# Block-sparse attention with a gated convolution: one tile for keys and queries, more buffers, and two segments' output turned on TensorE

## The chip, the cores and the metric

The kernel runs on one core of a Trainium2 chip. Time is device microseconds of that core for one launch, inputs in device memory at the start and the output there at the end. The time before is the median of three runs, 211.81 us (210.3 to 212.96).

The core has five engines that work side by side, each through its own queue in order, and meet at semaphores: TensorE (PE; the loading of its stationary operand is listed as PEld), VectorE (DVE), ScalarE (ACT), GpSimd (POOL) and SyncE (SP). SP and POOL here mainly issue DMAs.

## The reference

Attention of 4 batches x 8 heads, 768 positions, 64 elements a head, with a mask by blocks of 32; its output, heads side by side, goes through a feed-forward layer whose hidden values are gated by a short convolution over positions.

```python
scores = scale * np.matmul(q, k.transpose(0, 1, 3, 2))
mask = np.abs(blk_i - blk_j) <= window                  # neighbours, first and last block,
mask = mask | (blk_i == 0) | (blk_j == 0) | (blk_i == n_blocks - 1) | (blk_j == n_blocks - 1)
# ... and three sampled key blocks for each query block
attn = softmax(np.where(mask, scores, -1e9))
x = np.matmul(attn, v)            # -> (4, 768, 512), heads side by side
h = np.maximum(x @ w_in, 0.0)     # 512 -> 1024
conv_out = sum(conv_w[k] * shift(h, k - 1) for k in range(3))
out = (h * sigmoid(conv_out)) @ w_out
```

## The kernel before, in words

All 768 x 768 scores of a head are computed; the mask is added inside the same matmul, by 24 more rows of the contracted dimension (rows 64 to 87 of the key and query tiles, one row a block).

**Segments and units.** Heads are taken in pairs (16 pairs, named P). A batch has two query segments of 384 positions; the very last is cut in 256 and 128, so there are nine segments (`SEGS`). A segment's attention is cut in units: a unit is eight blocks of 128 keys x 128 queries, 144 units in all. For each unit TensorE computes scores into one of two `st` tiles (L744, two halves of four blocks), ScalarE takes the exponential into a `pt` tile (L755), and TensorE multiplies with the values into `av` (L777), where a column of ones gives the sum. When a pair of heads is done with a segment, VectorE takes the reciprocal of the sums (L694) and normalises into `xtok` (L696, both in `norm_ops`). `xtok` has positions on partitions; the next matmul needs features there, so it is transposed into `xT`: by a DMA through the crossbar, issued from SP (L705), or, for the (segment, pair) listed in `X_PE` (L217), by TensorE (L715) with a copy out of the `mix` tile.

**Feed-forward.** For each segment, 32 matmuls "f1" (L893) into `mix`, a rectifier on ScalarE or VectorE (L913, L915) into `hE`, the convolution as multiplications and additions on VectorE (L947, L957), tanh on ScalarE (L996), the gate on VectorE (L999, L1004) and the matmuls "f2" (L823), whose result goes through `o2s` to the output.

**Keys and queries.** For each pair, the key and query tiles stand as two: `E_t` and `O_t` (L156, L157), each with three blocks of 128 for keys and queries and two heads. A row of the loaded tile `nat` holds neighbouring positions, so the even and the odd of them come out of a transpose on partitions 0 to 63 and 64 to 127, and go to `E_t` and `O_t`. Pairs 0 to 4 are transposed on TensorE (L468, L506) and copied out of PSUM (`cp` in `kq_transposes`, through `dcopy`, L326 and L328); the others through the crossbar into `stg` (L583) and from there with two copies, "stg_cp". A score matmul takes the keys of one block and one or two neighbouring query blocks of the same tile. Slots 1 to 4 get their mask rows from slot 0 by copies on VectorE or DMAs on SP (L359); the last batch's second segment gets its own query rows by DMAs ("m_last", L595).

**Order.** Nothing is scheduled at run time. `put_down` walks the string `ORDER` (L20), which names each operation, the engine it goes to where there is a choice (ScalarE or VectorE for copies and rectifiers), and the buffer it takes; each engine's queue holds its operations in that order. GpSimd issues the loads (L238) with tiny copies "pace" between them (L415, L658) that wait for an exponential or an earlier load, so that loads do not run ahead.

Of the kernel before, what the change touches and what calls it, by code (L numbers as in the profile page):

```python
# [20 lines left out]
040708090506000b1e00a0A0102030e0c0z0d0gV1f1c01q11s11t0WV20f0hA0oA0UAr21r3r4r5r6r7r8r9rarbrcrdrerfrgrhrirjrkrl  # L21
rmrnrorprqrrrsrtru0Y0rv1210ZA00XA0VA0+ArwrxryrzrArBrCrDrErFrGrH0/015110A16A0i0x13V14V0lV0jVrI4o017A0y0mV11V0B
0nA4prJrK4t14q04u1g11hV11j01lV1kV0q0p1dV01E21G31H1801m11S00O1U2461V0t0u0w0v4v11iV4y04z4D14E4A24I04J4F34K44r14s
4w4Q14R4S54x4B4C0s0r1rV14V04W4G1u01vV24+14/4X05011x11zV4H4L1yV4N0530544M05b15c4T0E15525d31wV0C0F1FV25g05h1I04U
5l14Y5i45m1JV34Z1L11KV5n51MV1NV4O5q05r19051525v15w565s05x1571TV30G5810J0N591bV1aV5e15D05E5f5j5k5o5I15J5F25p5t
1n15N05u5y5O5z05G0P470Q48241490R4a1A04b0S4c2604d274e0T4f2c24g1O14h2e14i2f4j2k04k2m34P05a4l2n4m5K35S15H5L5T5P4
5A25B5C1oV5U55/05M605Q6105R6415V5W656906a5X05Y25V41pV5Z05+V6616e16216fhr1ho06b26g36j0hp636khs0k0DhqV0htVhM06l4
6r1676s6t5hx0hyhzA6w06xhu1hv1B06y0hOhNhPhwVhQhU1hVhWhX6B16C686c6d6hhD16G0hE6H1CA1DA6D1hFAhA06i6m6n06O1hB1W16u
6P6v6z6I2hCAhRhY1XV46o1i021YV6pi16Q36T0hG06A6U6E6V4hH6F6Y16ZhJ16J6+56KhK710726R16S6WhZhLAhIA730i3hSi26L0i4hT0
i57611P1im06X6/1RV1QV777e01Z1707f747817j17k756M2806q1296Ni831+V1/Viah+2dV0h/i9ig17g27l37o07p797a07h7i7t17u7q4  # L30
i6ibi77b2ic7v5ih7B07C7D0id7m7n7r7s7G17w7x7Hin2lV12aV0io7L07M2g12h7I17N2ii7c7d7y12bV7z7E17Q17R7F7J7K7V07Wieifip
7O7S37A7X42s12u2v24n0IiqV0811827P7T7U860878358807Y7Z0ij8b18civ0iw8g08h7+02iV12jV2tV2ixV7/ikA1is1itiuViQ08d12o0
# [80 lines left out]
def kernel(  # L113
# [90 lines left out]
    def t_d4(n):  # L204
        return 0.129 + n / 3840.0
# [855 lines left out]
```

## Time and profile before

| | |
|---|---|
| median of three runs | 211.81 us (210.3, 211.81, 212.96) |
| profiled execution: span from first to last instruction | 207.2 us |
| profiled execution: its own time beside the span | not listed apart; the median stands 4.6 us above the span |
| PE / PEld busy | 196.7 / 153.7 us |
| DVE / ACT / POOL busy | 181.5 / 189.4 / 60.7 us |
| exponentials on ScalarE (L755) | 144 of 1036 ns, 140.2 us busy |
| score matmuls (L744) | 900 |
| crossbar transposes of the attention output (SP) | 32 |
| read and written | 23.08 and 6.29 MB |

How to read it: PE's busy time counts matmuls that overlap in its pipeline, so their mean durations hold latency, and distances between starts say more about its rate. PEld runs beside PE. An idle time is put down to what ended last before it. A line can be that of a helper: all plain copies on VectorE are L328, all on ScalarE L326, all loads L238.

### The profile page before, as it was taken

How to read it: one execution, taken by the hardware profiler on the slowest of the kernel's cores; microseconds unless marked ns; L12 is line 12 of the kernel's file. 1: busy time of each engine (PE TensorE's matmuls, PEld its weight loads, DVE VectorE, ACT ScalarE, POOL GpSimd, SP SyncE). 2: the span in 40 equal slices, each digit the busy share in tenths (PEclk: the TensorE clock that was granted, in tenths of full speed). 3: DMA queues.
4: the chain of work that ended last, by engine and by line, in shares of the span. 5: the costliest groups of instructions: out<-in, count | busy, mean ns of one | idle time of the engine just before them, and what ended most of it. 6: DMA issues, size and time to landing. Idle time of an engine off the chain costs nothing.

```text
span 207.2 us, 6783 instructions
## 1 busy us (share of the span) xinstructions
PE 196.7 (95%) x2667; PEld 153.7 (74%) x2687; DVE 181.5 (88%) x571; ACT 189.4 (91%) x248; POOL 60.7 (29%) x113
## 2 busy tenths in 40 slices
PE   7799979989999999999999999999999999999993
PEld 7689858867878877777688767777688877795752
DVE  6877759999699998999999998999799959999950
ACT  6899969999999999999999998999899999998841
POOL 8844355446326124500605292700000000000000
PEclk9999999999999999999999999999999999999999
DMA  6999999999998699993597689992511032100415
GB/s 149 170 207 200 173 169 126 141 135 157 158 151 134 98 138 194 181 190 58 77 167 133 88 103 218 170 213 73 175 43 22 19 121 66 29 11 6 156 50 202
DMA packets 54903, 26.26 MB, mean 127 GB/s; under 512 B 40864, under 2 KB 51832, under 8 KB 54872
## 3 DMA queue, kind: packets, MB, share of 16 engines
q0 software_dynamic: 19984, 11.24, 43.5%
q1 hardware_dynamic: 34312, 13.90, 33.8%
q10 hardware_dynamic: 576, 0.69, 1.0%
q8 instruction: 21, 0.34, 0.7%
q14 instruction: 10, 0.08, 0.2%
HBM read 23.08 MB, written 6.29 MB: 142 GB/s over the span
## 4 chain that ended last, share of the span: by engine, by line
PE 56%; ACT 16%; DVE 16%; DMA 5%; issue 4%; SPq 0%; ACTq 0%
PE st L744 16%; PE mix L893 14%; PE mix L823 14%; ACT pt L755 12%; PE av L777 9%; DVE m L947 5%; DMA xT<-xtok 3%; DVE m L957 3%; DMA o2s<-in_q_dram 2%; DVE hE L915 2%; DVE xtok L696 2%; DVE gT L1004 1%; ACT hE L913 1%; DVE m L999 1%; DVE e L328 1%
## 5 line engine op out<-in xcount | busy, mean ns | idle before, releaser
L755 ACT ACTIVATE pt<-st 128x1024 bf16<-128x1024 f32 x144 | 140.2, 1036 | 5.4 <-PE st L744 5.0
L777 PEld LDWEIGHTS <-pt 128*128 128x128 bf16 x1152 | 53.1, 97 | 11.6 <-issue 0.2
L777 PE MATMUL av<-vt,pt 128*128 128x65 bf16 x1152 | 60.6, 193 | 0.3
L893 PE MATMUL mix<-xT,winb 128*128 128x384 bf16 (+2 forms) x288 | 53.8, 308 | 1.1 <-DMA xT<-xtok 0.9
L947 DVE TENSOR_SCALAR m<-hE,cw 128x382 bf16<-128x382 bf16 (+2 forms) x192 | 49.6, 317 | 0.2
L744 PE MATMUL st<-o 88*128 88x128 bf16 (+1 forms) x240 | 44.3, 229 | 1.1 <-ACT pt L755 0.8
L744 PE MATMUL st<-o,e 88*128 88x128 bf16 (+1 forms) x228 | 43.8, 233 | 0.5 <-ACT pt L755 0.4
L744 PE MATMUL st<-e,o 88*128 88x128 bf16 (+1 forms) x224 | 43.0, 234 | 1.2 <-ACT pt L755 1.2
L823 PE MATMUL mix<-woutb,gT 128*128 128x512 bf16 x156 | 43.1, 379 | 0.8
L744 PE MATMUL st<-e 88*128 88x128 bf16 (+1 forms) x208 | 41.5, 239 | 0.6 <-ACT pt L755 0.5
L744 PEld LDWEIGHTS <-o 88*128 88x128 bf16 x464 | 34.4, 97 | 9.4 <-issue 3.0
L744 PEld LDWEIGHTS <-e 88*128 88x128 bf16 x436 | 33.0, 97 | 7.5 <-issue 1.4
L957 DVE TENSOR_TENSOR m<-m 128x764 bf16<-128x764 bf16 (+2 forms) x64 | 33.8, 532 | 0.4
L893 PEld LDWEIGHTS <-winb 128*128 128x128 bf16 x288 | 23.9, 97 | 8.2 <-issue 1.6
L996 ACT ACTIVATE m<-m 128x764 bf16<-128x764 bf16 (+2 forms) x32 | 26.3, 826 | 0.5 <-DVE m L957 0.4
L415 POOL COPY pace<-pt 1x1 bf16<-1x1 bf16 x24 | 8.3, 347 | 47.3 <-ACT pt L755 47.0
L823 PEld LDWEIGHTS <-gT 128*128 128x128 bf16 x184 | 15.4, 97 | 9.0 <-DVE gT L1004 0.5
L915 DVE TENSOR_SCALAR hE<-mix 128x384 bf16<-128x384 f32 x29 | 15.9, 554 | 4.3 <-PE mix L893 4.1
L696 DVE TENSOR_TENSOR xtok<-av,rcp 128x384 bf16<-128x384 f32 (+2 forms) x36 | 18.2, 506 | 0.3
L1004 DVE TENSOR_TENSOR gT<-m,hE 128x764 bf16<-128x764 bf16 (+3 forms) x36 | 18.1, 508 | 0.3
L913 ACT ACTIVATE hE<-mix 128x384 bf16<-128x384 f32 (+2 forms) x35 | 16.9, 503 | 1.6 <-PE mix L893 1.2
L238 POOL DMA_DIRECT2D nat<-in_q_dram x23 | 16.9, 736 | 3.0 <-issue 2.8
(80 smaller groups left out, 156.4 us busy)
## 6 DMA issues: line engine op xcount, KB each, us to landing
out_dram<-o2s SPq DMA_DIRECT2D x22, 256.0 KB
vn<-in_v_dram POOLq DMA_DIRECT2D x16, 192.0 KB, 5.3
nat<-in_k_dram POOLq DMA_DIRECT2D x15, 192.0 KB, 5.1
nat<-in_q_dram POOLq DMA_DIRECT2D x7, 192.0 KB, 4.8
winb<-in_moe_w_in_dram POOLq DMA_DIRECT2D x2, 512.0 KB, 8.1
woutb<-in_moe_w_out_dram POOLq DMA_DIRECT2D x4, 256.0 KB, 5.8
nat<-in_q_dram POOLq DMA_DIRECT2D x8, 96.0 KB, 5.3
xT<-xtok SPq DMA_TRANSPOSE x32
```

The lines of the kernel that those rows point to most:

```text
L696: nm = op("norm", {"DVE": t_dps(128 * C)}, lambda e: nc.vector.tensor_tensor(out=xtok_t[xk.index][:, 0:C].rearrange("p c h d -> p h c d"), ...
L744: nc.tensor.matmul(out=st[:, 128 * x:128 * (x + n_)], lhsT=QK[kc % 2][s][0:88, 1, hh, kc // 2, :], rhs=QK[par][s][0:88, 0, hh, idx:idx + n ...
L755: nc.scalar.activation(out=pt_t[ptb.index], in_=st_t[stb.index], func=AF.Exp, bias=0.0, scale=0.125)
L777: nc.tensor.matmul(out=o[:, off:off + 65], lhsT=pt_t[ptb.index][:, 128 * x:128 * x + 128], rhs=V_t[vslot_b[P].index][:, hh, kc, 0:65], sta ...
L823: nc.tensor.matmul(out=acc(), lhsT=gT_t[gb.index][:, ffc, 128 * t:128 * t + 128], rhs=woutb[:, ffc, :], start=(ffc == 0), stop=(ffc == NFF ...
L893: nc.tensor.matmul(out=mix_t[hb.index][:, w1 * y:w1 * y + w1], lhsT=winb[:, fc, 128 * ffc:128 * ffc + 128], rhs=xT_t[xt_buf[n].index][:, f ...
L913: i = nc.scalar.activation(out=dst, in_=src, func=AF.Relu, bias=0.0, scale=0.5)
L915: i = nc.vector.tensor_scalar(out=dst, in0=src, scalar1=0.5, scalar2=0.0, op0=ALU.mult, op1=ALU.max)
L947: i = nc.vector.tensor_scalar(out=m_t[cb.index][:, x, y, 0:w], in0=hE_t[heb.index][:, f0 + y, t0 + x:t0 + x + w], scalar1=cw[:, x, f0 + y: ...
L957: nc.vector.tensor_tensor(out=m[:, a_, :, 0:w], in0=m[:, a_, :, 0:w], in1=m[:, b_, :, 0:w], op=ALU.add)
L996: th = [op("tanh", {"ACT": t_act(2 * w) + 0.04}, lambda e, cb=cb, w=w: nc.scalar.activation(out=m_t[cb.index][:, 0, :, 0:w], in_=m_t[cb.in ...
L1004: i = nc.vector.tensor_tensor(out=gT_t[gtb.index][:, f0:f0 + 2, t0:t1], in0=m_t[cb.index][:, 0, :, 0:w], in1=hE_t[heb.index][:, f0:f0 + 2, ...
```

## The change

- Keys and queries of a pair stand in one tile `QK_t` with six blocks; `E_t` and `O_t` become views of every second block. The blocks of a query segment are thereby neighbours (0, 1, 2 and 3, 4, 5), and a score matmul takes up to three of them. Mask rows are copied in fewer, larger pieces; `mlast`'s three parts change places to fit.
- More buffers: `stg` 2 to 3, `nat` 4 to 6, `vn` 3 to 4, `pt` 6 to 8, `xtok` and its sums 3 to 4, `xT` 3 to 4, `o2s` 4 to 5.
- `X_PE` also names all four pairs of segments 0 and 1.
- `ORDER` is another string: other places in the queues, other engines for some copies, other buffers.

```diff
@@ -151,10 +152,10 @@
     av_t = [ps.tile([128, 512], FP32, tag=f"av{x}", name=f"av{x}") for x in range(NAV)]
     mix_t = [ps.tile([128, 512], FP32, tag=f"mix{x}", name=f"mix{x}") for x in range(NMIX)]
 
-    NSLOT, NSTG, NNAT, NVN, NPT, NXK, NXT, NHE, NCV, NGT, NOS = 5, 2, 4, 3, 6, 3, 3, 2, 4, 2, 4
-
-    E_t = many(NSLOT, [88, 2, 2, 3, 128], BF16, "e")
-    O_t = many(NSLOT, [88, 2, 2, 3, 128], BF16, "o")
+    NSLOT, NSTG, NNAT, NVN, NPT, NXK, NXT, NHE, NCV, NGT, NOS = 5, 3, 6, 4, 8, 4, 4, 2, 4, 2, 5
+
+    QK_t = many(NSLOT, [88, 2, 2, 6, 128], BF16, "qk")
+    E_t, O_t = [[t[:, :, :, x:6:2] for t in QK_t] for x in range(2)]
     V_t = many(NSLOT, [128, 2, 6, 66], BF16, "vt")
     stg_t = many(NSTG, [128, 2, 2, 3, 128], BF16, "stg")
     nat_t = many(NNAT, [128, 2, 768], BF16, "nat")
@@ -214,7 +215,7 @@
 
     SW = 0.715
     NWARM = 45
-    X_PE = ((0, 3), (7, 3), (8, 2), (8, 3))
+    X_PE = ((0, 0), (0, 1), (0, 2), (0, 3), (1, 0), (1, 1), (1, 2), (1, 3), (7, 3), (8, 2), (8, 3))
     WOUT_U = (15, 19, 23, 27)
 
 
@@ -316,7 +317,7 @@
         put(to[:, 1:2, :, 5:11], 1)
         mid = to[:, 0:1, :, 6:11]
         a_ = [list(x) for x in mid.ap]
-        put(bass.AP(tensor=mid.tensor, offset=mid.offset, ap=[a_[0], [255, 2], [16, NB // 3], [1, 5]]), 1)
+        put(bass.AP(tensor=mid.tensor, offset=mid.offset, ap=[a_[0], [511, 2], [16, NB // 3], [1, 5]]), 1)
 
     def k_copy(t, h):
         return lambda e: dcopy(e, t[0][64:88, 1, h], E_t[0][64:88, 1, 0])
@@ -334,7 +335,7 @@
     mlast = sb.tile([88, 3, 128], BF16, tag="mlast", name="mlast")
 
     def last_rows(e):
-        for y, (t0, c, n_) in enumerate(((384, 0, 2), (640, 0, 1), (384, 1, 2))):
+        for y, (t0, c, n_) in enumerate(((384, 0, 2), (384, 1, 2), (640, 0, 1))):
             src = nblk[:, t0:t0 + 128 * n_].rearrange("j (p c) -> j c p", c=n_)[:, c]
             if e == "ACT":
                 nc.scalar.activation(out=mlast[64:88, y], in_=src, func=AF.Copy, bias=0.0, scale=-8000.0)
@@ -351,13 +352,12 @@
     mask_ready[(0, 1)] = m_h1 + m_kh
     for s in range(1, NSLOT):
         mr = []
-        for x, t in enumerate((E_t, O_t)):
-            if s < SLOT_DMA:
-                mr.append(op("m_slot", {"DVE": t_d4(1536) + 0.05}, lambda e, t=t, s=s: dcopy(e, t[s][64:88], t[0][64:88]),
-                             T(4.5 * s - 2.5) + 0.1 * x, [m_h1[x], m_kh[x]], earliest=7.0 + 2 * s))
-            else:
-                mr.append(op("m_dma", {"SP": 0.75}, lambda e, t=t, s=s: nc.sync.dma_start(out=t[s][64:88], in_=t[0][64:88]),
-                             T(4.5 * s - 2.5) + 0.1 * x, [m_h1[x], m_kh[x]], dma=("hw", 0.6)))
+        for x, t in enumerate((E_t, O_t) if s < SLOT_DMA else ()):
+            mr.append(op("m_slot", {"DVE": t_d4(1536) + 0.05}, lambda e, t=t, s=s: dcopy(e, t[s][64:88], t[0][64:88]),
+                         T(4.5 * s - 2.5) + 0.1 * x, [m_h1[x], m_kh[x], m_k[x]], earliest=7.0 + 2 * s))
+        if s >= SLOT_DMA:
+            mr = 2 * [op("m_dma", {"SP": 0.75}, lambda e, s=s: nc.sync.dma_start(out=QK_t[s][64:88], in_=QK_t[0][64:88]),
+                         T(4.5 * s - 2.5), m_h1 + m_kh + m_k, dma=("hw", 0.6))]
         mask_ready[(s, 0)] = mask_ready[(s, 1)] = mr
 
     def mask_in(slot, h, kp, par):
@@ -482,7 +482,7 @@
             for x, t in enumerate((E_t, O_t)):
                 def cp(e, t=t, x=x, hs=hs, mb=mb, n=n, bt=bt):
                     src = bt[mb.index].bitcast(BF16)[64 * x:64 * x + 64, 384 * hs[0]:384 * hs[0] + n]
-                    dcopy(e, t[slot.index][0:64, 1, hs[0]:hs[-1] + 1].rearrange("p h c s -> p (h c s)"), src)
+                    dcopy(e, t[slot.index][0:64, 1, hs[0]:hs[-1] + 1], src.rearrange("p (h c s) -> p h c s", h=len(hs), c=3))
                 a = {"DVE": t_d2(n) + 0.06, "ACT": t_act(n)}
                 cps.append(op("k_cp", a, cp, pr + 0.5 + 0.1 * x, [tr],
                               alloc=[slot] if (P, 0, "k") not in qk_ready and x == 0 else [],
@@ -592,10 +592,9 @@
                           after=[slot_first.get(P - 1)] if x == 0 and P == NSLOT else []))
         mr = []
         if b == B - 1:
-            for t, at, x0, n_ in ((O_t, 0, 1, 2), (E_t, 2, 2, 1)):
-                mr.append(dma("m_last", "SP", lambda t=t, x0=x0, n_=n_: t[slot.index][64:88, 0, :, x0:x0 + n_],
-                              mlast[64:88, at:at + n_].unsqueeze(1).broadcast_to([NB, 2, n_, 128]), due + 12, [o_ml],
-                              service=0.05, uses=[slot]))
+            mr.append(dma("m_last", "SP", lambda: QK_t[slot.index][64:88, 0, :, 3:6],
+                          mlast[64:88].unsqueeze(1).broadcast_to([NB, 2, 3, 128]), due + 12, [o_ml],
+                          service=0.05, uses=[slot]))
         for h in range(2):
             for g in range(2):
                 qk_ready[(P, h, g)] = [[[cps[kp], cps[par]] + mask_in(NSLOT - 1, 0, kp, par) + (mr if g else [])
@@ -661,7 +660,7 @@
 
     kc_order = [0, 2, 4, 1, 3, 5]
 
-    blk_order = {0: [(0, 0, 0), (0, 1, 2), (1, 0, 1)], 1: [(1, 1, 0), (1, 2, 2), (0, 2, 1)]}
+    blk_order = {0: [(0, 0, 0), (1, 0, 1), (0, 1, 2)], 1: [(1, 1, 0), (0, 2, 1), (1, 2, 2)]}
 
     SEGS = [(n // 2, n % 2, 384 * (n % 2), 3, blk_order[n % 2]) for n in range(NHALF - 1)]
     SEGS += [(B - 1, 1, 384, 2, [(1, 1, 0), (0, 2, 1)]), (B - 1, 1, 640, 1, [(1, 2, 0)])]
@@ -677,7 +676,6 @@
                         blocks.append((4 * b + hp, hh, kc, par, idx, c))
         for i in range(6 * C):
             units.append((n, blocks[8 * i:8 * i + 8]))
-    QK = [E_t, O_t]
     av_buf, av_last, norm, xtr, xt_buf = {}, {}, {}, {}, {}
     prev_s = prev_av = None
     all_s = []
@@ -729,23 +727,24 @@
             for x, (P, hh, kc, par, idx, c) in enumerate(bls):
                 if (P, hh) not in heads:
                     heads.append((P, hh))
-                if pieces and pieces[-1][:4] == (P, hh, kc, par) and pieces[-1][4] + pieces[-1][6] == idx:
-                    pieces[-1] = pieces[-1][:6] + (pieces[-1][6] + 1,)
+                at = 2 * idx + par
+                if pieces and pieces[-1][:3] == (P, hh, kc) and pieces[-1][3] + pieces[-1][5] == at:
+                    pieces[-1] = pieces[-1][:5] + (pieces[-1][5] + 1,)
                 else:
-                    pieces.append((P, hh, kc, par, idx, 4 * part + x, 1))
+                    pieces.append((P, hh, kc, at, 4 * part + x, 1))
             deps = []
             for (P, hh, kc, par, idx, c) in bls:
                 deps += [d for d in qk_ready[(P, hh, g)][kc % 2][par] if d not in deps]
 
             def s_fn(e, stb=stb, pieces=pieces):
                 st = st_t[stb.index]
-                for (P, hh, kc, par, idx, x, n_) in pieces:
+                for (P, hh, kc, at, x, n_) in pieces:
                     s = slot_b[P].index
                     nc.tensor.matmul(out=st[:, 128 * x:128 * (x + n_)],
-                                     lhsT=QK[kc % 2][s][0:88, 1, hh, kc // 2, :],
-                                     rhs=QK[par][s][0:88, 0, hh, idx:idx + n_, :].rearrange("p c s -> p (c s)"),
+                                     lhsT=QK_t[s][0:88, 1, hh, kc, :],
+                                     rhs=QK_t[s][0:88, 0, hh, at:at + n_, :].rearrange("p c s -> p (c s)"),
                                      start=True, stop=True)
-            prev_s = op("s", {"PE": sum(t_mm(128 * p[6]) for p in pieces)}, s_fn, T(u) - 1.2 + 0.3 * part, deps, after=[prev_s],
+            prev_s = op("s", {"PE": sum(t_mm(128 * p[5]) for p in pieces)}, s_fn, T(u) - 1.2 + 0.3 * part, deps, after=[prev_s],
                         lat=0.262, alloc=[stb] if part == 0 else [],
                         uses=[slot_b[P] for P in sorted({h[0] for h in heads})] + ([stb] if part else []))
             s_ops.append(prev_s)
```

The two strings of `ORDER` are left out; they say nothing to a reader.

More of the change, by code (lines that the diff above doesn't have):

```diff
@@ L56 @@
[L56 to L60 removed]
+040708000b1c01d010z0203r31r4r5r6r7r8r9rarbrcrdrerfrgrhrirjrkrlrmrn0905060a1a01600w0v0e0c0hV0d0x0oV0f0gArorprq
@@ L61 @@
+gEgF3gQ5ocodA2gM0gW0gXoggNoQ1gGgY6gH0ohgRgIAoigS1ps0pth21paoTp3oUgT0oVgUojV4h3h70gZpp1g+oWpuApbh42oXp4pcg/2pJ2
+h0gV0h1okoepqh8prApv0pwh91h50h6py1pzpKpB1oYpLpxAhahg1hhpj0hb1pAAhc1hdhi7he1pkplpmhfApMpDpZ0pNpChjhkpnA0pd1pe
+hl3hmpOhn0pfpR3pEhoApgpTpSpFpPpUp/qn0qophA3qpApiqk1qlpGqq0qrqD0qmApHpVqEqsApIpWpQqh1qiqy1qzq50q6p+qF1qA2qjAqI0
+qJqb1qt1quqcq0q1pXqBq2pYq3qGqv3qdq7q4qeqwqxqK0qN0qHqLqCqOqfV1qMq8qT1qPqQq9V4qaqgpoqRA2qSAqUqVqWqZ0qXV3qYSq+q/
+r0r1Ar2A
 """
```

75 lines of the change are left out of this document (35 added, 40 removed).

## Prediction

> **What bounds the kernel now.** I read the profile from the coarse to the fine: the busy shares, the waits, then the order of time on one engine.
>
> ```profile
> span 207.2 us, 6783 instructions
> PE 196.7 (95%) x2667; PEld 153.7 (74%) x2687; DVE 181.5 (88%) x571; ACT 189.4 (91%) x248; POOL 60.7 (29%) x113
> ...
> PEclk9999999999999999999999999999999999999999
> ```
>
> Three engines lie between 88% and 95%, so no single one explains the time; the clock of TensorE (PEclk) is full throughout. The waits say who starved whom. Their columns are the waiter, the releaser, the total in us, how often, and the longest:
>
> ```profile
> ACT pt L755 <- PE st L744: 5.0, 11, 1.6
> ...
> PE st L744 <- ACT pt L755: 3.0, 8, 1.2
> ...
> PE mix L893 <- DMA xT<-xtok: 0.9, 1, 0.9
> ...
> PEld L715 <- DVE xtok L696: 0.5, 2, 0.3
> ```
>
> ScalarE's exponentials waited only 5.0 us in all for scores, so ScalarE is close to gapless. Its own order of time, then the chain that ended last (start, length, what):
>
> ```profile
> 8.03 0.51 ACT L326 COPY e<-e 24x384 bf16<-24x384 bf16 x1
> 8.57 20.79 ACT L755 ACTIVATE pt<-st 128x1024 bf16<-128x1024 f32 x22
> 30.91 1.94 ACT L755 ACTIVATE pt<-st 128x1024 bf16<-128x1024 f32 x2 [1.55 <-PE st L744]
> ```
> ```profile
> 22.73 6.50 DMA xT<-xtok
> 29.27 0.65 PE mix L893 x3
> ...
> 77.28 0.44 PE st L744 x6
> ...
> 138.40 0.48 PE av L777 x16
> ...
> 161.00 0.45 PE st L744 x8
> ```
>
> From 8.57 us, 22 exponentials run without a break, 20.79/22 = 0.945 us each. They begin straight behind a small copy on ScalarE (8.03). Then comes the largest hole in them, 1.55 us before the one at 30.91, and the chain shows its cause: the first feed-forward matmuls begin at 29.27, when a crossbar transpose of the attention output lands 6.50 us after 22.73; the score matmuls stand behind them in TensorE's queue. One unit of attention costs TensorE 0.44 (scores) + 0.48 (attention times value) = 0.92 us against 0.945 on ScalarE, so TensorE can hardly catch up a hole. VectorE by windows (busy us of ten: PE, PEld, DVE, ACT):
>
> ```profile
> 10.00:20.00 10.00, 9.15 (x156) 8.42 (x154) 7.90 (x21) 10.00 (x12) 4.63 (x8) 1.00 1.33 203
> 20.00:30.00 10.00, 8.60 (x153) 7.35 (x151) 6.71 (x28) 9.24 (x10) 4.33 (x10) 1.00 1.32 176
> 30.00:40.00 10.00, 9.84 (x142) 7.96 (x141) 9.17 (x27) 9.03 (x13) 4.81 (x11) 1.00 1.27 131
> 40.00:50.00 10.00, 9.06 (x147) 7.48 (x148) 9.45 (x30) 10.00 (x14) 6.22 (x10) 1.00 1.23 137
> ```
>
> It has 2.1 us free from 10 to 20, 3.3 from 20 to 30, but only 0.8 and 0.5 in the next two.
>
> **The wide tile.** Blocks 0, 1, 2 of a query segment become neighbours, so a score unit of 1024 columns, six matmuls now (eight in the last segment's units), takes four. Over the kernel 900 score matmuls become 600, with the same columns. The chain has 0.44 us for x6 and 0.45 for x8: two more matmuls cost 0.01 after rounding, that is 0 to 10 ns each. I take 2 ns, near the lower end, since loading and matmul of a piece of 128 already follow each other without a gap in both rows: 300 x 2 ns = **-0.6 us** of TensorE, bounds 0 and -3.0. The mask DMAs on SP's queue go from 12 to 6; no engine waits for them in the waits, so 0, and fewer can't come later.
>
> The copies into the tile now write pieces of 128 elements with gaps of 128 between them.
>
> ```profile
> L328 DVE COPY o<-stg 64x1536 bf16<-64x1536 bf16 x11 | 6.5, 595 | 0.3
> ...
> L328 DVE COPY vt<-vn 128x768 bf16<-128x768 bf16 x16 | 5.6, 359 | 0.1
> ...
> L328 DVE COPY o<-mix 64x768 bf16<-64x768 bf16 x4 | 2.2, 558 | 0.1
> ```
>
> The value copy (vt) already writes runs of 64 into rows of 66, and takes 359 ns for 768 elements; the gapless stage copy takes 595 for twice as many, so 236 ns for the second 768. A fixed part of 123 and 0.307 ns an element fit both: a gap costs nothing there. I take 0 for the 22 stage copies and 4 mask copies. The other end: at the rate of the copy from PSUM (558 for 768, that is 0.56 ns an element behind the same fixed part) a copy of 1536 would take 0.99 us, +0.39 each, 26 x 0.39 = +10.1.
>
> **The attention output by TensorE.** Of the first two segments' eight transposes, seven go from SP's queue (27 whole ones become 20) to TensorE: 7 x 3 = 21 transposes there, and 7 copies out of PSUM, all on VectorE in the changed order.
>
> ```profile
> 7.71 0.50 PE L468 MATMUL mix<-ident,nat 128*128 128x128 bf16 x6
> ```
> ```profile
> L328 DVE COPY xT<-mix 128x384 bf16<-128x384 bf16 x1 | 0.4, 358 | 0.0
> ...
> L715 PE MATMUL mix<-ident,xtok 128*128 128x128 bf16 x7 | 1.1, 220 | 0.0
> ```
>
> Six transposes fill 0.50 us while one alone lasts 0.22, so (0.50 - 0.22)/5 = 56 ns each in a row: 21 x 0.056 = **+1.2 us** of TensorE, and 7 x 0.358 = **+2.5** of VectorE. [...]
>
> What it buys: the first f1 group no longer waits for 22.73 + 6.50. In the changed order it stands where it stood, behind score unit 21, with the fourth head pair's transposes four attention matmuls behind that pair's last one (before: directly behind). The hole of 1.55 us should shrink to what eight f1 matmuls in a row leave: 8 x 0.65/4 = 1.3 us of f1 and 0.44 of scores against the two exponentials (1.9) that run meanwhile, so 0 to 0.5. **-1.3 us** taken, bounds -1.55 and 0.
>
> What is late next? On POOL's queue the weights of f1 now stand behind two more loads, and pair 2's keys behind two loads of later queries:
>
> ```profile
> 4.47 0.75 POOL L238 DMA_DIRECT2D nat<-in_k_dram  x1
> ...
> 13.84 0.35 PEld L468 LDWEIGHTS <-nat 128*128 128x128 bf16 x6
> ...
> 16.20 0.77 POOL L238 DMA_DIRECT2D winb<-in_moe_w_in_dram  x1
> ```
> ```profile
> nat<-in_k_dram POOLq DMA_DIRECT2D x15, 192.0 KB, 5.1
> ...
> winb<-in_moe_w_in_dram POOLq DMA_DIRECT2D x2, 512.0 KB, 8.1
> ```
>
> Pair 2's keys are issued at 4.47 and land 5.1 later, near 9.6, and are read at 13.84; two more issues of 0.75 make it 11.1, still covered. The second half of the weights is issued at 16.20 and lands near 24.3; the first half, put directly ahead of it, lands about then too, 3 us before its first use near 27.5. Both cost nothing; without that cover the hole stays and the gain is 0, which is the bound above. On SP's queue the stage transposes now stand ahead of all transposes of the attention output; those of the first two segments, which would have been held up there, are gone.
>
> The wait that is added: a transpose on TensorE waits for VectorE's normalised output, and the score matmuls behind it wait too, then the exponential. The nearest row is the last of the waits quoted: 0.3 at the longest. By the changed order six of the eight stand 24 to 56 attention matmuls behind what they need; two stand 4 and 0 behind: 2 x 0.3 = 0.6 at most, which I count in the range, as before had one such too.
>
> **The head.** Three mask copies and two query copies of the first pair go from ScalarE to VectorE.
>
> ```profile
> 6.12 0.35 ACT L326 CAST nat<-o2s 128x192 bf16<-128x192 f32 x1 [0.50 <-DMA o2s<-in_q_dram]
> 6.50 0.47 ACT L326 COPY o<-mix 64x384 bf16<-64x384 bf16 x1
> ...
> 7.00 0.74 ACT L326 COPY e<-av 64x384 bf16<-64x384 bf16 x2
> ```
>
> Behind the cast at 6.12 ScalarE has two copies of 384 left, some 0.9 us by these rows, so the first exponential may begin near 7.4 instead of 8.57: -1.2. But VectorE takes about 1.4 us more before it prepares pair 1, and that pair's first scores come at unit 4, where the start gained is mostly waited away; VectorE's 2.1 us free by 20 us let it recover a part. I take the middle, **-0.6**, bounds -1.2 and 0.
>
> **Buffers and the new order.** More buffers remove waits only where a buffer was late; loads then come earlier. Counted by work alone, up to exponential 60 the changed order has TensorE 2.3 us further on (1.2 of it transposes) and ScalarE level within 0.4 us; behind it TensorE has 1.7 us less to do, ScalarE 0.5 less, VectorE the same kinds.
>
> ```profile
> 60.00:70.00 10.00, 10.00 (x160) 8.31 (x159) 9.88 (x30) 10.00 (x14) 3.79 (x5) 1.00 0.85 126
> ...
> 150.00:160.00 10.00, 10.00 (x153) 8.19 (x151) 9.93 (x32) 9.75 (x13) 0.00 (x0) 1.00 0.16 36
> ```
>
> All three are full there, so the smaller saving and the larger bound it: **-1.0**, bounds -1.7 and 0. Against it the four copies of the second segment fall where VectorE has 0.8 and 0.5 free: 4 x 0.358 = 1.4 and some mask work, beyond the cover by **+0.6** (0 to 2.5). TensorE's own +1.2 - 0.6 lies within its 2.3 ahead and is not counted again. The tail (last segments) keeps its order but for two output copies that change engines: 0.
>
> Sum: -1.3 - 0.6 - 1.0 + 0.6 = -2.3 us on a span of 207.2, so 204.9. What lies around the span isn't shown; the median, 211.81, stands 4.6 above it. With that kept: **209.5 us**. A measurement here tells about 2% (4.2 us) from no change; its three runs spread over 2.7.
>
> **The rivals.**
> (a) All waits of ScalarE for scores go, 5.0 us instead of 1.3 of them, with the head's -1.2: 207.2 - 6.2 gives 205.6 at best. For it: buffers and an earlier start of feed-forward. Against: those waits after 80 us come from TensorE being full. 203.5 to 207.5.
> (b) Slower: VectorE takes the pace. By the count of the orders it gets 7 copies more, less two smaller ones, two output evictions for two rectifiers, and the mask and query copies of the head: about +3.7 us. If it is full from 8 to 60 us, all of that is time, and each of the eight transposes then waits 0.3 us (+2.4), with scores and exponentials behind: 211.8 + 1 to + 6, so 213 to 217.5. It decides once VectorE's windows from 30 to 60 all stand above 9.8 us. For it: 9.17 and 9.45 now; against: 3.3 us free just before.
> (c) The gapped copies run at the PSUM rate: +10.1 of VectorE, partly in its free time, 217 to 222. Against it stands the vt row.
> (d) Loading of weights is what bounds TensorE:
>
> ```profile
> L744 PEld LDWEIGHTS <-o 88*128 88x128 bf16 x464 | 34.4, 97 | 9.4 <-issue 3.0
> L744 PEld LDWEIGHTS <-e 88*128 88x128 bf16 x436 | 33.0, 97 | 7.5 <-issue 1.4
> ```
>
> 900 loads hold 67.4 us, so 300 fewer would free 22.5; ScalarE's 207.2 - 189.4 = 17.8 us of idle time let at most that through, so 194 to 203.5. [...] But sixteen loads and matmuls pass in 0.48 us (av), 30 ns each, so loads hide behind matmuls.
> That the change doesn't do what it says is the 0 bound of the transposes: weights late instead of the crossbar, 210.8, within the forecast's case.
>
> **How the numbers follow.** Forecast 0.43 (207.6 to 212), (a) 0.20, (b) 0.24, (c) 0.10, (d) 0.03. Faster by over 2% is below 207.6: (a) and (d), 0.23. Slower by over 2% is above 216.0: (c) and half of (b), 0.22. Within: 0.55. The range 203.5 to 217.5 leaves out (d) and most of (c), with edges of (a) and (b).
>
> **What would show it.** The profile after should have the first exponential near 7.4 to 8, no hole over 0.5 us before the 23rd, the transposes on TensorE at 56 ns, stage copies below 0.62 us, score units at 0.44, and VectorE under 9.8 from 30 to 60. A stage copy of 0.99 proves (c); a longer wait of TensorE for xtok than 0.3, (b). I am wrong altogether if the full stretch from 80 to 190 us changes by more than 2 us, since nothing that I counted acts there.

## The result, and the profile after

The median of 20 executions is 208.31 us (207.43 to 210.4), against 211.3 us (208.78 to 214.03) for 20 of the kernel before, taken beside them. The ratio is 0.9913 [0.9885, 0.9941]: 0.9% faster, and not by the 2% that would count as a change here. The ratio is taken over the executions within 1.5% of their kernel's fastest, which leaves out the longest ones of the kernel before; the two medians stand 1.4% apart. The forecast was 209.5 us. The profiled execution took 208.25 us, 206.5 of it span. The first lines of the page after:

```profile
span 206.5 us, 6207 instructions
PE 197.2 (96%) x2391; PEld 142.9 (69%) x2408; DVE 184.6 (89%) x583; ACT 188.6 (91%) x245; POOL 59.3 (29%) x113
...
PEclk9999999999999999999999999999999999999999
```

Against the page of before, TensorE has 0.5 us more of work, VectorE 3.1 more, ScalarE 0.8 less, and the span is 0.7 shorter. The waits (waiter, releaser, total in us, times, longest) and ScalarE's order of time (start, length, what, idle before it) say where that came from:

```profile
ACT pt L754 <- PE st L743: 1.9, 8, 0.4
...
PEld L713 <- DVE xtok L694: 0.2, 1, 0.2
...
PE mix L892 <- DMA xT<-xtok: 0.2, 1, 0.2
```
```profile
7.46 3.88 ACT L754 ACTIVATE pt<-st 128x1024 bf16<-128x1024 f32 x4 [0.20 <-PE st L743]
...
11.50 15.29 ACT L754 ACTIVATE pt<-st 128x1024 bf16<-128x1024 f32 x16 [0.17 <-PE st L743]
27.05 1.94 ACT L754 ACTIVATE pt<-st 128x1024 bf16<-128x1024 f32 x2 [0.25 <-PE st L743]
```

The exponentials begin at 7.46 instead of 8.57, the hole of 1.55 us is now 0.25, and ScalarE's wait for scores fell from 5.0 to 1.9. The wait that was added, a transpose on TensorE for the normalised output, is 0.2 in all. The costs, from the groups (busy us, mean ns of one | idle before) and TensorE's order of time:

```profile
L329 DVE COPY qk<-stg 64x1536 bf16<-64x1536 bf16 x22 | 12.0, 549 | 0.2
...
L329 DVE COPY xT<-mix 128x384 bf16<-128x384 bf16 x8 | 2.8, 355 | 0.8 <-PE mix L713 0.6
```
```profile
19.89 0.33 PE L713 MATMUL mix<-ident,xtok 128*128 128x128 bf16 x3
```

The gapped copy takes 549 ns, no more than the 595 of before; the copy out of PSUM takes 355; three transposes take 0.33, which is 0.22 for the first and 0.055 for each further one. VectorE by windows (PE, PEld, DVE, ACT, POOL, then clock, DMA share, GB/s):

```profile
20.00:30.00 10.00, 9.88 (x142) 7.65 (x139) 7.63 (x28) 9.62 (x12) 3.70 (x8) 1.00 0.99 147
30.00:40.00 10.00, 9.49 (x133) 7.05 (x131) 9.83 (x30) 9.90 (x15) 4.05 (x9) 1.00 1.12 149
40.00:50.00 10.00, 8.90 (x127) 6.71 (x125) 9.59 (x27) 9.47 (x12) 4.89 (x11) 1.00 1.16 151
50.00:60.00 10.00, 10.00 (x117) 7.08 (x115) 9.86 (x34) 9.74 (x13) 3.21 (x6) 1.00 0.90 111
```

From 30 to 60 us VectorE is now at 9.83, 9.59 and 9.86 of ten, so it has little room left there. The start of the same exponential in both profiles says how far each kernel is:

| exponential | before | after | gained |
|---|---|---|---|
| 0 | 8.57 | 7.46 | 1.11 |
| 6 | 14.01 | 13.33 | 0.68 |
| 16 | 23.49 | 22.67 | 0.82 |
| 24 | 33.10 | 31.58 | 1.52 |
| 30 | 42.66 | 40.34 | 2.32 |
| 42 | 55.19 | 54.65 | 0.54 |
| 60 | 75.89 | 75.61 | 0.28 |
| 78 | 99.66 | 97.11 | 2.55 |
| 102 | 129.95 | 127.71 | 2.24 |
| 120 | 154.19 | 153.84 | 0.35 |
| 143 (last) | 189.28 | 188.05 | 1.23 |

Of the 1.52 at exponential 24, 0.82 was there by exponential 16, ahead of the hole; from there to behind the hole 0.7 more is gained. Further down the column rises and falls, but it does not show time won and lost alone, because the two orders put other work between the same exponentials. Counted by the weights that TensorE has loaded, at exponential 60 the changed kernel has 21 transposes and 7 "f2" matmuls more behind it and 8 "av" fewer, some 2.5 us by an estimate from what each takes in the traces (0.056, 0.22 and 0.03 us); at exponential 78 it has 4 "f2" and 17 "av" fewer, some 1.4 us. At the end of the span 0.7 is left.

**One thing the profile of before did not show.** The granted clock of TensorE is recorded for every execution, and it is not the same in all of them. Of the 93 executions of the kernel before that ran beside the experiments below, on three chips, only 14 had the full clock (0.996 or more), with spans from 206.6 to 209.2 and a mean of 207.9 us; 44 had 0.987 to 0.995 and a mean of 208.6; 35 had less and a mean of 211.0. The mean of all is 209.4. Of the changed kernel's 20, 14 had the full clock, with 205.6 to 207.9 and a mean of 206.5, and six 0.987 to 0.995, with 207.4: mean 206.8. At full clock the change is worth 207.9 - 206.5 = 1.4 us (by the spread of these, within 0.5 or so; the five of each with a clock of 1.000 stand closer, at 207.2 and 206.8); on the mean of all it is worth 2.6. The 1.2 between the two comes with executions in which the clock fell, most of it with the longest of them: without 24 of the longest of the kernel before, 0.3 of it is left. That the fall itself costs all of this is not shown: in the segment-1 run below the clock falls in the middle of a wait of 6.96 us, which costs time by itself. The profiled execution of before, at 207.2, was one of the few without a fall, and one of the shorter of those. (A clock just under 1 need not mean a fall that matters: the profile of the segment-0 run below, with 0.997, is below full clock only from 205.7 us of its 206.8 on.)

### The profile page after: what moved, and what is told of

It is laid out like the page before. It is cut to its first block, busy times and chain, and to the rows that moved or that the text cites. A ratio compares the mean times of both kernels' runs of the same rounds, so it can differ in the third digit from the quotient of the medians.

```text
span 206.5 us, 6207 instructions
## 1 busy us (share of the span) xinstructions
PE 197.2 (96%) x2391; PEld 142.9 (69%) x2408; DVE 184.6 (89%) x583; ACT 188.6 (91%) x245; POOL 59.3 (29%) x113
## 4 chain that ended last, share of the span: by engine, by line
PE 72%; DVE 16%; ACT 5%; DMA 3%; issue 2%; SPq 0%; ACTq 0%; DVEq 0%
PE st L743 24%; PE mix L892 16%; PE mix L822 14%; PE av L776 14%; DVE m L946 5%; DVE qk L329 4%; ACT pt L754 3%; DVE m L956 3%; DMA xT<-xtok 2%; DMA sbi<-in_sampled_blocks_dram 1%; DVE xtok L694 1%; PE mix L807 1%; PE st L822 1%; DVE m L998 1%; PE av L967 1%
## 5 line engine op out<-in xcount | busy, mean ns | idle before, releaser
L743 PE MATMUL st<-qk 88*128 88x256 bf16 (+2 forms) x600 | 89.1, 267 | 2.4 <-ACT pt L754 1.2
L743 PEld LDWEIGHTS <-qk 88*128 88x128 bf16 x600 | 48.3, 97 | 22.2 <-issue 3.7
L776 PE MATMUL av<-vt,pt 128*128 128x65 bf16 x1152 | 59.3, 193 | 0.3
L822 PE MATMUL mix<-woutb,gT 128*128 128x512 bf16 x159 | 43.8, 379 | 0.6
L912 ACT ACTIVATE hE<-mix 128x384 bf16<-128x384 f32 (+2 forms) x37 | 18.2, 496 | 1.1 <-PE mix L892 0.8
L914 DVE TENSOR_SCALAR hE<-mix 128x384 bf16<-128x384 f32 x27 | 14.6, 550 | 3.8 <-PE mix L892 2.7
L329 DVE COPY qk<-mix 64x256 bf16<-64x256 bf16 (+4 forms) x28 | 11.1, 403 | 2.2 <-PE mix L468 1.3
L998 DVE TENSOR_SCALAR m<-m 128x764 bf16<-128x764 bf16 (+3 forms) x36 | 11.9, 337 | 1.0 <-ACT m L995 0.8
L329 DVE COPY qk<-stg 64x1536 bf16<-64x1536 bf16 x22 | 12.0, 549 | 0.2
L239 POOL DMA_DIRECT2D vn<-in_v_dram x16 | 11.5, 716 | 2.2 <-DVE m L956 1.0
```

Of the source, the lines that this page charges most:

```text
L239: return op(name, {eng: occ}, lambda e: on(e).dma_start(out=dst(), in_=src), prio, deps, dma=(kind, service), **kw)
L329: nc.vector.tensor_copy(out=dst, in_=src)
L743: nc.tensor.matmul(out=st[:, 128 * x:128 * (x + n_)], lhsT=QK_t[s][0:88, 1, hh, kc, :], rhs=QK_t[s][0:88, 0, hh, at:at + n_, :].rearrange( ...
L776: nc.tensor.matmul(out=o[:, off:off + 65], lhsT=pt_t[ptb.index][:, 128 * x:128 * x + 128], rhs=V_t[vslot_b[P].index][:, hh, kc, 0:65], sta ...
L822: nc.tensor.matmul(out=acc(), lhsT=gT_t[gb.index][:, ffc, 128 * t:128 * t + 128], rhs=woutb[:, ffc, :], start=(ffc == 0), stop=(ffc == NFF ...
L912: i = nc.scalar.activation(out=dst, in_=src, func=AF.Relu, bias=0.0, scale=0.5)
```

## The experiments

The expectations set the prediction's own account (the hole and the later start are what was gained) against one in which VectorE's room set the time, and, in two of the last four runs, one by TensorE's clock. The kernel before ran beside each set; ratios are to it. The changed kernel did not run beside them, and the kernel before at full clock differs by 0.5 us among the three chips (207.7 to 208.3), so a few tenths between a run's mean and the changed kernel's are not clear of noise. Lines in the experiments' profiles are shifted: in most, the exponential is L763, the first feed-forward matmuls L901, the scores L752.

### One segment back on the crossbar

Three runs keep the changed order and put transposes back on SP, in the place that the order gives to TensorE's, and leave out the copy. First segment 0 (its fourth pair, which TensorE already turned before, stays):

```diff
+            back = (n, hp) in ((0, 0), (0, 1), (0, 2))
...
+                if back:
+                    nc.sync.dma_start_transpose(out=xT_t[xb.index][:, hp, 0:128 * C]...,
+                                                in_=xtok_t[xk.index][:, 0:C]...)
+                    return
```

> The changed kernel, with the first three head pairs of segment 0 turned by the crossbar again, issued from SP where TensorE's transposes stood. Theory A (the gain is the hole ahead of the 23rd exponential, kept to the end): the hole of about 1.5 us is back and the end is 1 to 1.5 us later, ratio 0.996 to 0.999 of before. Theory B (the early gain is eaten by VectorE before 60 us, what remains comes from the head and the order): the hole is back, the end moves by less than 0.5 us, ratio 0.990 to 0.994.

Ratio 0.9935 [0.9905, 0.9966], median 208.84; span 206.8 in the profile and 206.8 on the mean of 8 executions of 12 with full clock (changed kernel: 206.5). In its order of time on ScalarE and its chain the crossbar's hole is back:

```profile
30.31 0.49 ACT L921 ACTIVATE hE<-mix 128x384 bf16<-128x384 f32 x1 [1.29 <-PE mix L901]
```
```profile
23.81 5.28 DMA xT<-xtok
29.14 1.14 PE mix L901 x6
```

Exponential 24 starts 1.53 us later than in the changed kernel, 60 starts 1.27 later, 102 1.09, 120 and the last 0.60, and the span is 0.3 longer. As the order is otherwise the same, these numbers compare place by place. The hole is real and is what the prediction said, but of the 1.5 us gained at it 0.3 to 0.6 reach the end. The trace of the changed kernel shows two places where the rest goes. TensorE waits there for transfers, and in this run, which is later, it does not:

```profile
40.63 0.40 PE L506 MATMUL mix<-ident,nq 128*128 128x128 bf16 x4 [0.20 <-DMA nq<-in_q_dram]
...
147.39 0.97 PE L892 MATMUL mix<-xT,winb 128*128 128x384 bf16 x5 [0.18 <-DMA xT<-xtok]
```

Behind the first, a load of queries, the changed kernel's lead falls from 1.53 to 1.28 (exponential 31); behind the second, a later crossbar transpose, from 1.09 to 0.60 (117 and 118). The lead is taken back where something comes no earlier. What the turn's own work costs, nine transposes (0.5 us of TensorE) and three copies (1.07 us of VectorE), is not separated here.

For segment 1 the tuple is `((1, 0), (1, 1), (1, 2), (1, 3))`:

> The changed kernel, with segment 1's four pairs turned by the crossbar again. VectorE is freed of four copies of 358 ns between 30 and 45 us, TensorE of 12 transposes. Theory B (VectorE is full there and takes the pace): the exponentials from the 36th on come 0.7 to 1.4 us earlier, the end 0.5 to 1 us earlier, ratio 0.986 to 0.989. Rival (VectorE's fullness there costs nothing, or the crossbar's 5 to 6.5 us are late for f1 of segment 1): no gain or a loss, ratio 0.991 to 0.998.

Ratio 1.0248 [1.0189, 1.0307], median 215.93. None of its six executions had the full clock. The profiled one is the longest of them, with a span of 216.5 us against 214.2 on the mean, and its granted clock is 0.50, half of full, from 43.8 to 47.2 and from 57.4 to 67.6 us. In it exponential 36 is 1.8 us late, behind the first of these stretches, and 42 8.8 us. Its order of time on ScalarE, and its chain:

```profile
63.46 1.02 ACT L763 ACTIVATE pt<-st 128x1024 bf16<-128x1024 f32 x1 [6.96 <-PE st L752]
```
```profile
47.01 8.46 DMA nat<-in_q_dram
55.47 0.02 SPq L586
...
56.82 4.84 DMA xT<-xtok
61.67 0.04 issue
61.71 0.80 PE mix L901 x2
```

A load of later queries lands at 55.47; only then does SP get past the stage transpose that waits for it (L586), and the attention output's transpose behind it lands at 61.66. TensorE meanwhile stands still (busy for 0.00 us of the four from 57 to 61), so the relief of VectorE that the run was made for cannot be read from it. Most of this size is the price of SP's order, not of the crossbar as such: in that order the stage transposes stand ahead, and segment 1 can no longer be turned there.

> The changed kernel with both segments' seven pairs through the crossbar: the wide tile, buffers and order stay. Theory A: the sum of the two, hole back, +0.5 to +1.5 us, ratio 0.994 to 0.999. Theory B: the loss of the hole and the relief of VectorE cancel, within 0.5 us of the changed kernel, ratio 0.989 to 0.994.

Both tuples together: 1.0048 [1.0003, 1.0094], median 213.26; exponential 42 starts 7.4 us late, and three executions of 12 had the full clock. The two parts do not add up (0.2% and 3.4% lost against the changed kernel apart, 1.4% together); why both are cheaper than segment 1 alone was not taken further.

### The wide tile

Every score matmul cut to 128 columns again, 1152 instead of 600:

```diff
-                if pieces and pieces[-1][:3] == (P, hh, kc) and pieces[-1][3] + pieces[-1][5] == at:
+                if False:
```

> The changed kernel with every score block as a matmul of its own on the same wide tile: 1152 score matmuls for 600, same columns. If the fixed part of a matmul is 2 ns, TensorE has 1.1 us more, and the end moves by 0 to 1.1 us, ratio 0.991 to 0.997. If it is near the upper bound of 10 ns, 5.5 us more, ratio 1.01 to 1.02, and the wide tile would be worth 3 us by itself.

Ratio 0.9949 [0.9916, 0.9982], median 208.48. The span is 207.1 in the profile (+0.6), and 206.63 on the mean of 10 executions with full clock (+0.14). For 552 more matmuls that is 0.3 to 1.1 ns each at the end of the kernel; by that, 300 fewer are worth 0.1 to 0.3 us. Loading of weights went from 142.9 to 157.7 us of PEld, so rival (d) is out.

The wide tile alone on the old order (its diff is that of the change, without buffers, `X_PE`, `ORDER` and the merged mask pieces; the last batch's mask rows go in four DMAs a pair):

> The kernel before with the wide tile alone: one key and query tile, blocks in the order 0, 1, 2, score matmuls merged to 600, all else and the order as before (the last batch's mask rows go in 16 small DMAs for 8). If merging is worth 2 ns a matmul: -0.6 us of TensorE, ratio 0.996 to 1.000. If gapped copies cost nothing, the stage copies stay near 580 ns; if they run at the PSUM rate, near 990 ns and the ratio is above 1.02.

Ratio 0.9959 [0.9925, 0.9994], median 210.92. One execution of 12 had the full clock, much as before. The 22 stage copies, now with gaps, take 589 ns. By this run's interval the tile is worth 0.1 to 1.6 us, by the one above 0.1 to 0.3; that one keeps the tile and the order and changes the matmuls alone, and is the sharper.

### Turning segment 0 on the old order

```diff
+            if n in SEGS_TURNED:
+                def turn(x):
+                    t = mix_t[x].bitcast(BF16)
+                    for c in range(C):
+                        nc.tensor.transpose(out=t[:, 128 * c:128 * c + 128], in_=xtok_t[xk.index][:, c]..., identity=ident)
+                    dcopy("DVE", xT_t[xb.index][:, hp, 0:128 * C], t[:, 0:128 * C])
```

The three pairs are turned two score halves after their normalisation, in a free `mix` tile; all else keeps its place.

> The kernel before with segment 0's other three head pairs turned by TensorE, two half units of scores behind their normalisation, copies on VectorE, all else in the old order. Theory A: the hole of 1.55 us ahead of the 23rd exponential goes to under 0.5, and the end is 0.8 to 1.3 us earlier, ratio 0.993 to 0.997. Theory B: the hole goes and the end moves by less than 0.5 us, ratio 0.998 to 1.002.

Ratio 0.9956 [0.9927, 0.9985], median 208.95, and 8 of 12 executions with the full clock (before, beside it: 4 of 34), mean span there 207.1 against 208.0: 0.9 us less at full clock, of the 1.9 by which the mean span of all is shorter. But the profile does not bear out the account by the hole. Its 1.55 us have become three waits of 1.84 us in all (the exponential is L796 here, the scores L785):

```profile
25.85 1.02 ACT L796 ACTIVATE pt<-st 128x1024 bf16<-128x1024 f32 x1 [0.49 <-PE st L785]
27.70 2.92 ACT L796 ACTIVATE pt<-st 128x1024 bf16<-128x1024 f32 x3 [0.83 <-PE st L785]
31.14 1.94 ACT L796 ACTIVATE pt<-st 128x1024 bf16<-128x1024 f32 x2 [0.52 <-PE st L785]
```

The turned pairs stand so close behind their normalisation that TensorE waits for VectorE, 0.6 us for the normalised output and 0.4 for the copy out of `mix`. Exponential 24 starts 0.23 us later than before, and both profiles have a span of 207.2. So where the 0.9 comes from no trace shows, and it rests on eight executions against four.

### Buffers alone, and the head alone, on the old order

```diff
-    NSLOT, NSTG, NNAT, NVN, NPT, NXK, NXT, NHE, NCV, NGT, NOS = 5, 2, 4, 3, 6, 3, 3, 2, 4, 2, 4
+    NSLOT, NSTG, NNAT, NVN, NPT, NXK, NXT, NHE, NCV, NGT, NOS = 5, 3, 6, 4, 8, 4, 4, 2, 4, 2, 5
```

(with each operation given the buffer that has been free longest)

> The kernel before with the changed kernel's numbers of buffers, each operation taking the buffer that has been free longest, in the old order. If buffers matter only with an order made for them: ratio 0.998 to 1.002. If waits for buffers hold the old order up: below 0.997.

Ratio 0.9988 [0.9951, 1.0025]: more buffers by themselves do nothing that stands clear of noise.

```diff
+            if not started and o.name in ('m_h1', 'q_cp') and e == 'ACT':
+                e = 'DVE'
```

> The kernel before with two mask copies and two query copies of the first pair moved from ScalarE to VectorE, as in the changed kernel. The first exponential near 7.5 instead of 8.57. If the head's gain is kept as far as VectorE allows: the sixth exponential 0.3 to 0.7 us earlier, the end as much, ratio 0.996 to 0.998. If the full stretch behind takes it: ratio 0.999 to 1.001.

Ratio 1.0066 [1.0021, 1.0112], slower. The first exponential begins at 9.33, later than the 8.57 of before:

```profile
9.33 1.94 ACT L759 ACTIVATE pt<-st 128x1024 bf16<-128x1024 f32 x2 [2.15 <-PE st L748]
```

Two mask and two query copies moved from ScalarE to VectorE, with VectorE's queue as it was, put the first scores behind VectorE's other work. None of its 11 executions had the full clock, so a part of the loss may be the clock's. The earlier start of the changed kernel comes from that queue's new order, not from the change of engine: the run with the old head, below, begins its first exponential at 7.47 with such copies on ScalarE.

### The clock

That TensorE's clock falls where TensorE has been quiet was the author's guess, and the next two runs were made to test it. Where does TensorE go quiet? Windows of one us from 8 to 12 us, of the kernel before and then of the changed one (us busy of PE, PEld, DVE, ACT, POOL, then the clock):

```profile
8.00:9.00 1.00, 0.43 (x8) 0.31 (x6) 0.74 (x2) 0.95 (x3) 1.00 (x3) 1.00 1.18 164
9.00:10.00 1.00, 0.36 (x5) 0.34 (x5) 0.95 (x3) 1.00 (x2) 0.52 (x1) 1.00 1.37 187
10.00:11.00 1.00, 0.69 (x10) 0.53 (x8) 0.94 (x3) 1.00 (x2) 0.00 (x0) 1.00 1.35 194
11.00:12.00 1.00, 0.69 (x11) 0.50 (x9) 0.96 (x2) 1.00 (x2) 0.73 (x2) 1.00 1.29 192
```
```profile
8.00:9.00 1.00, 0.93 (x13) 0.62 (x11) 0.97 (x5) 1.00 (x2) 1.00 (x3) 1.00 1.38 189
9.00:10.00 1.00, 0.91 (x7) 0.47 (x6) 0.97 (x3) 1.00 (x2) 1.00 (x2) 1.00 1.42 196
10.00:11.00 1.00, 0.42 (x3) 0.19 (x2) 0.94 (x3) 1.00 (x2) 0.97 (x3) 1.00 1.39 192
11.00:12.00 1.00, 0.90 (x14) 0.67 (x14) 0.94 (x4) 0.83 (x2) 1.00 (x3) 1.00 1.38 199
```

From 8 to 12 us TensorE is busy 2.17 us before and 3.16 after (the first number behind the width, summed). The next run gives the changed kernel its old head: the second head's two query copies and two of the mask copies are back on ScalarE.

```diff
+    late_q = [o for o in ops if o.name == 'q_cp'][2:4]
...
+            if o.name == 'm_h1' or o in late_q:
+                e = 'ACT'
```

> The changed kernel with the two query copies and two mask copies of the first pair's second head on ScalarE again: the second exponential some 1.1 us later. Theory C: the quiet stretch of TensorE and with it the fall of the clock are back in many runs, mean 1 to 2 us above the changed kernel, ratio 0.995 to 1.000. If the head is worth only its start: 0.3 to 0.7 us above it, ratio 0.993 to 0.996, clock as in the changed kernel.

Ratio 0.9965 [0.9931, 0.9999], median 209.87. Four executions of 12 had the full clock (mean span 207.2, +0.7 on the changed kernel); the others had 208.6 on the mean. In the profile the first exponential begins at 7.47, as in the changed kernel, and the second, behind the copies, 1.34 later. The fall is in it:

```profile
9.00:10.00 1.00, 0.26 (x3) 0.24 (x3) 0.72 (x3) 0.95 (x3) 1.00 (x2) 1.00 1.33 175
10.00:11.00 1.00, 0.44 (x5) 0.14 (x3) 0.94 (x3) 1.00 (x2) 1.00 (x4) 1.00 1.36 181
11.00:12.00 1.00, 0.68 (x7) 0.43 (x6) 0.97 (x3) 1.00 (x2) 0.95 (x3) 0.96 1.36 190
12.00:15.00 3.00, 3.00 (x28) 2.25 (x27) 1.58 (x3) 2.62 (x3) 2.29 (x4) 0.50 1.32 216
```

TensorE, at 0.26 to 0.68 for three us, drops to half clock (0.50) near 11.9 and comes back near 15.3. So the head is worth 0.7 us at equal clock, and 4 of 12 executions at full clock against 14 of 20 suggest that it bears on the falls too. Then 28 matmuls that nobody reads were added to the kernel before, in the quiet stretch:

```diff
+FILL = {4: 16, 6: 6, 8: 6}
...
+            nc.tensor.matmul(out=av_t[0][:, 0:128], lhsT=warm, rhs=warm, start=True, stop=True)
```

> The kernel before with 28 matmuls more that nobody reads, in TensorE's quiet stretch: 16 ahead of the scores of unit 2, 6 ahead of those of units 3 and 4 each (1.5 us in all, where TensorE waits for exponentials). Theory C (TensorE's clock falls for 3.4 us after the quiet stretch of 8 to 12 us, in most executions of the old kernel, and that is half of the gain): granted clock 0.996 or more in most runs, mean time 0.7 to 1.5 us less, ratio 0.993 to 0.997, runs closer together. Rival (the clock falls for another reason, or costs nothing since TensorE waits anyway): ratio 0.999 to 1.003.

Ratio 1.013 [1.0096, 1.0165], slower, and none of six executions with the full clock. In the profile the head no longer falls: the clock is 1.00 up to 28 us. The fall has gone elsewhere, as the chain and the windows of the profile show:

```profile
22.56 9.14 DMA xT<-xtok
31.75 1.12 PE mix L901 x3
```
```profile
28.00:30.00 2.00, 1.05 (x14) 0.83 (x15) 0.82 (x3) 1.20 (x2) 1.06 (x3) 0.74 1.69 138
30.00:32.00 2.00, 0.59 (x2) 0.10 (x1) 0.75 (x6) 0.03 (x1) 0.38 (x1) 0.50 1.96 92
32.00:34.00 2.00, 2.00 (x13) 1.24 (x12) 0.03 (x1) 0.00 (x0) 1.44 (x4) 0.50 0.64 105
34.00:36.00 2.00, 2.00 (x19) 1.53 (x17) 1.28 (x4) 1.02 (x1) 1.14 (x3) 0.55 0.92 105
```

The crossbar transpose before the first feed-forward took 9.14 us here, against 6.50 in the profile of before; from 26 to 32 us TensorE was busy for 0.77, 1.05 and 0.59 of two us each, and its granted clock was 0.50 from near 29 to near 35.8. So the head is not the only place where the clock falls: here it falls at the hole, and the change fills both.

Which of them makes the falls is not decided. The kernel before has one in 79 of 93 executions, and the changed kernel with its old head in 8 of 12. But with segment 0 turned on the old order, where the head keeps the order of before, it is 4 of 12, and with the hole back in the changed kernel also 4 of 12, against 6 of 20 without it. So neither a quiet head nor the hole brings by itself the falls of the kernel before. Why the transpose took 2.6 us longer in this kernel was not found either.

### What TensorE's and VectorE's new work costs

The transposes of the first two segments done twice, 24 more:

```diff
-                for c in range(C):
+                for c in 2 * list(range(C)) if n < 2 else range(C):
```

> The changed kernel with each of the 24 transposes of the first two segments on TensorE done twice: 24 x 0.056 = 1.3 us more of TensorE between 15 and 43 us, nothing else. If TensorE's work is paid wherever it stands (theory D: the full stretch behind sets the end): end 0.8 to 1.4 us later than the changed kernel, ratio 0.994 to 0.998. If TensorE's lead there covers it, as the prediction had it: 0 to 0.4 us, ratio 0.991 to 0.993.

Ratio 0.9931 [0.9904, 0.9958]. In the profile exponential 36 starts 1.48 us later and the last 1.16, by the 24 x 0.056 = 1.3 us that they hold TensorE; but on the mean of the seven executions with full clock the span is 206.6, 0.1 more than without them. Profile and mean disagree, and what TensorE's 1.2 us cost at the end stays open between 0.1 and 1.

And the eight copies done twice (2.9 us more of VectorE):

```diff
+                for _ in range(2 if n < 2 else 1)], due, [pt_],
```

> The changed kernel with each of the eight copies of the first two segments' transposes out of PSUM done twice on VectorE: 8 x 0.358 = 2.9 us more of VectorE. If VectorE is the pace from 30 to 50 us: the exponential number 36 1 to 1.4 us later, the end 0.7 to 1.5 us later, ratio 0.994 to 0.999. If VectorE's free time covers it: end within 0.4 us, ratio 0.991 to 0.993.

Ratio 0.9986 [0.9957, 1.0015]. Exponential 36 starts 0.28 later, 42 1.13 and 60 1.56, the last 0.89, and the span of the profile is 0.8 longer; the mean span of seven executions with full clock is 207.9, 1.4 more. Between a quarter and a half of VectorE's extra work there is paid.

## Why the prediction was right

The sign, the size and the class held: 0.9% faster was measured, 1.1% forecast. By its terms:

- **The hole, -1.3:** right in cause and at its place (1.55 to 0.25; with segment 0 back on the crossbar exponential 24 is 1.53 later), too large in what it is worth. The segment-0 run shows that 0.3 to 0.6 of it reaches the end.
- **The head, -0.6:** right in size. Exponential 0 starts at 7.46 (7.4 forecast), exponential 6 is 0.68 earlier, and giving the head back costs 0.7 at equal clock. The condition was missed: without a new order of VectorE the same move loses (1.0066).
- **The wide tile, -0.6:** mis-sized, 0.1 to 0.3 by the split; of the 2 ns a matmul half or less arrives at the end.
- **Gapped copies, 0:** right (549 ns). Rival (c) falls on this row, and (d) on the split.
- **The turn's own work:** 56 ns was right for transposes in a row, 0.358 for the copy. "TensorE's own +1.2 lies within its 2.3 ahead and is not counted again" stays open: 24 more transposes, 1.3 us, cost 0.1 on the mean of the executions with full clock and 1.2 by the last exponential of the one profile.
- **VectorE beyond the cover, +0.6:** about right or too small. Of 2.9 us added there 0.8 to 1.4 is paid, and the turn adds 2.5, so by an estimate at that rate 0.7 to 1.2. Rival (b) was partly right: its mark, 9.8 in all windows from 30 to 60, is reached in two of three. Its further price, 0.3 us of waiting for each transpose, is not there (0.2 in all).
- **Buffers and order, -1.0:** buffers alone 0. From exponential 60 to the last the gain goes from 0.28 to 1.23, which is the size taken, but with 2.5 in between, so it is not the level run that the mark of 2 us from 80 to 190 us assumed; that mark also speaks against the term itself, which is worked out from less work in that stretch. No run prices the new order alone.
- **What lies around the span, 4.6:** wrong. The profiled execution after has 208.25 - 206.5 = 1.75, and the kernel before has 1.8 on the mean of the experiments' runs. The other 2.8 was the spans themselves: the median of three was set beside a profile without a fall, and a short one, 0.7 below the mean of those at full clock. The clock of the three is not on record; spans near 210.0, as the median's less 1.8, were in the experiments' runs those of executions with falls.

The last point is the step that failed: "the clock of TensorE (PEclk) is full throughout" was true of one execution and taken for the kernel. 206.5 against the 204.9 forecast for the span is 1.6 too little gained at full clock (the hole's rest first, then the tile); the 2.8 around the span went the other way. The median forecast missed by only 2.8 - 1.6 = 1.2 us because two errors nearly cancelled, which is luck.

By the runs, the hole of segment 0 is worth 0.3 to 0.6 us, the head 0.7, the wide tile 0.1 to 0.3 and the buffers nothing: 1.1 to 1.6 together, against 1.4 at full clock. Each was taken alone, and the runs with segments 0 and 1 show that parts need not add up. What segment 1's turn is worth is not shown, since the run that takes it back measures SP's queue.

## What to carry to other kernels

Where executions of one kernel spread by 2%, look at the granted clock of each before working from one profile: the profiled one may be the exception, and the difference between its time and the span says which part of the median is not in it. A hole early in a kernel can be worth less than its length, where a load or a transfer that comes no earlier takes the lead back (here 1.5 us at its place and 0.3 to 0.6 at the end). With another order, the start of the same instruction in two profiles says little unless the work done up to it is counted too. To move a copy to an engine with free time was worth something here only with that engine's queue in a new order.

## What the runs showed of the hardware

TensorE's granted clock fell to 0.50 for 3.4 us in the profile of the run with the old head (near 11.9 to 15.3) and for 6.8, twice as long, in that of the run with the head's copies on VectorE (near 9.7 to 16.5); the run with segment 1 on the crossbar has a fall of 3.4 and one of 10.2. Executions of the kernel before whose mean clock is 0.987 to 0.995 (the profile of the run with the old head, with that one fall in its windows up to 66 us, has 0.988) are 0.6 us longer than those without a fall, and those below 0.987 are 3.0 longer, waits included.

In the run with the old head the clock fell behind three us in which TensorE was busy for 0.26, 0.44 and 0.68 of each. It need not fall, though: the profiled execution of the kernel before, with 0.43, 0.36, 0.69 and 0.69 in four us, kept the full clock (1.00 in all windows from 6 to 20 us).

Also unexpected: 552 more matmuls, each with its own load of weights, cost under a microsecond, while 28 small ones in the quiet head of the kernel before went with 1.3% more, in the profile with a crossbar transfer 2.6 us longer, which they do not touch.
